# Retiling the expert stage of an mLSTM and hash-routing kernel: 416 rows for each expert, row tiles and a shared column-tiled tile

## The chip, the cores and the metric

The kernel runs on one core of a Trainium2 chip. The metric is device time in microseconds (us) of one execution. All arithmetic that matters here is f32.

## The reference

Two blocks follow each other. The first is an mLSTM cell over 4 batches, 8 heads, 768 steps and a head size of 40; its output is bridged to 3072 tokens of 320 numbers. The second sends every token to one of 8 experts, a two-layer network of 320 to 1024 to 320:

```python
def _moe_ref(x, token_ids, w1, w2):          # x 3072x320, w1 8x320x1024, w2 8x1024x320
    expert_idx = token_ids * np.int64(2654435761) % np.int64(E)
    out = np.zeros((N, D), dtype=np.float32)
    for e in range(E):
        mask = expert_idx == e
        if not mask.any():
            continue
        xe = x[mask]
        h = np.maximum(xe @ w1[e], 0.0)
        out[mask] = h @ w2[e]
    return out.astype(np.float32)
```

The multiplier is 1 modulo 8, so a token's expert is its id modulo 8. With the ids that the reference's setup draws, the experts get 405, 404, 389, 366, 385, 370, 377 and 376 tokens.

## The kernel before

**The mLSTM stage** works by chunks of 128 steps, 24 chunks in all, and writes each chunk's 128 tokens to a buffer in HBM (`x_d`). Between the chunks, routing runs in pieces: every token gets a slot (expert, rank within the expert), and a table of slots becomes two index tiles, `g_idx` (which row of `x_d` a slot reads) and `s_idx` (which row of the output it writes). `route_slots` is the piece that turns ranks into slots on VectorE. An empty slot reads row 0 and writes beyond the output, which drops it.

**The expert stage** gives each expert NJ = 4 tiles of 128 slots, 512 rows. For each expert in turn:

- `gather`: four indirect DMAs on GpSimd's queue fetch 128 rows of 320 numbers each.
- `turn`: TensorE transposes each 128x320 tile in three pieces (128, 128 and 64 columns) into PSUM; VectorE copies the two full pieces to `xT`, ScalarE the 64-row piece.
- `layer1`: for each of FB = 8 blocks of 128 hidden units, three matmuls accumulate 512 columns in one PSUM bank: contraction rows 0 to 127, 128 to 255 and the remaining 64. VectorE (even blocks) and ScalarE (odd blocks) apply the relu into `h`.
- `layer2`: for each of the 4 tiles, eight matmuls with a 128x128 piece of `h` as weights and 320 columns of `w2t` moving; ScalarE copies the result, and an indirect DMA on GpSimd's queue scatters the rows.

TensorE's program in this stage is the plain loop: `layer1(e)`, `turn(e + 1)`, `layer2(e)`, with the gathers two experts ahead and the weights three. Each f32 matmul stands in the profile as two records, each with a weight load (engine PEld) of its own; a transpose is one record. After the eight experts a loop runs over tiles of tokens beyond an expert's capacity; with the counts above it has no iteration.

Two places of the mLSTM stage are used below because they already use part of the array: `scores` (L253) multiplies from partitions 0 to 39 for even heads, then from 64 to 103 for odd heads, and `state` (L273) writes head by head to output partitions 0 to 63 and 64 to 127 in turn.

Of the kernel before, what the change touches and what calls it, by code (L numbers as in the profile page):

```python
# [8 lines left out]
F32 = mybir.dt.float32  # L9
# [4 lines left out]
AF = mybir.ActivationFunctionType  # L14
# [8 lines left out]
def kernel(  # L23
# [41 lines left out]
    NJ = 4  # L65
    CAP = NJ * P
    NX = -(-(N - CAP) // P)
    NC = E * NJ + NX

    consts = ctx.enter_context(tc.tile_pool(name="consts", bufs=1))  # L70
    wpool = ctx.enter_context(tc.tile_pool(name="wpool", bufs=3))

# [7 lines left out]
    def weights(src1, src2):  # L80
        w1t = wpool.tile([P, DB, F], F32, name="w1t")
        w2t = wpool.tile([P, FB, Dm], F32, name="w2t")
        for db, (d0, dsz) in enumerate(dch):
            nc.sync.dma_start(w1t[:dsz, db, :], src1[d0 : d0 + dsz, :])
        nc.sync.dma_start(w2t[:], src2.rearrange("(a p) d -> p a d", p=P))
        return w1t, w2t
# [6 lines left out]
    with tc.tile_pool(name="gates", bufs=1) as gp, \  # L93
# [117 lines left out]
        def decays(s):  # L211
# [27 lines left out]
            # The sigmoid is below the least normal number where this bound on its exponent matters.  # L239
# [77 lines left out]
        # The routing depends on the token ids alone: it runs in pieces between the steps above.  # L317
        iotas = {}
        for name, shape, pattern, base, mult in (
            ("experts", [P, E], [[1, E]], 0, 0),  # L320
            ("b1off", [P, E], [[CAP, E]], -1, 0),
            ("b2off", [P, E], [[-CAP, E]], E * CAP - CAP, 0),
            ("thr", [P, NX], [[P, NX]], CAP, 0),
            ("kx", [1, NX], [[1, NX]], 0, 0),
            ("iota_f", [P, P], [[1, P]], 0, 0),
            ("tokv", [P, NT], [[1, NT]], 1, NT),
        ):
# [3 lines left out]
        experts, b1off, b2off, thr, kx, iota_f, tokv = (t[1] for t in iotas.values())  # L331
# [25 lines left out]
        def route_counts():  # L357
            # 2654435761 is 1 modulo E, so the hash is the id's low bits, of either sign and with any wrap.
# [40 lines left out]
        def route_slots():  # L399
# [3 lines left out]
            nc.vector.tensor_scalar(gx[:], slot[:], scalar1=CAP + 0.5, scalar2=None, op0=ALU.is_ge)  # L403
            nc.vector.tensor_tensor(gx[:], gx[:], b2[:].unsqueeze(2).to_broadcast([P, E, NT]), op=ALU.mult)
            nc.vector.tensor_add(slot[:], slot[:], gx[:])
# [36 lines left out]
        def route_index():  # L442
            # A slot without a token reads row 0 and writes beyond the last row, which drops it.
# [32 lines left out]
    def gather(g):  # L476
        g["xg"] = xp.tile([P, NJ, Dm], F32, name="xg", bufs=3)
        for j in range(g["n"]):
            nc.gpsimd.indirect_dma_start(  # L479
                out=g["xg"][:, j, :], out_offset=None,  # L480
                in_=x_d[:, :], in_offset=bass.IndirectOffsetOnAxis(ap=g["gi"](j), axis=0),
            )

    def turn(g):
        g["xT"] = xp.tile([P, DB, CAP], F32, name="xT")
        for j in range(g["n"]):
            tp = mps.tile([P, DB, P], F32, name="tp")
            for db, (d0, dsz) in enumerate(dch):
                nc.tensor.transpose(tp[:dsz, db, :], g["xg"][:, j, d0 : d0 + dsz], ident[:])
            full = [db for db, (_, dsz) in enumerate(dch) if dsz == P]  # L490
            nf = len(full)
            cols = slice(j * P, (j + 1) * P)
            nc.vector.tensor_copy(g["xT"][:, :nf, cols], tp[:, :nf, :])  # L493
            if nf < DB:
                dsz = dch[-1][1]
                nc.scalar.copy(g["xT"][:dsz, nf, cols], tp[:dsz, nf, :])

    def layer1(g):
        cols = g["n"] * P
        g["h"] = xp.tile([P, FB, CAP], F32, name="h")  # L500
        for fb in range(FB):
            hp = mps.tile([P, CAP], F32, name="mh", bufs=3)
            for db, (_, dsz) in enumerate(dch):
                nc.tensor.matmul(  # L504
                    hp[:, :cols], lhsT=g["w"][0][:dsz, db, fb * P : (fb + 1) * P], rhs=g["xT"][:dsz, db, :cols],
                    start=(db == 0), stop=(db == DB - 1),
                )
            if fb % 2 == 0:
                nc.vector.tensor_relu(g["h"][:, fb, :cols], hp[:, :cols])  # L509
            else:  # L510
                nc.scalar.activation(g["h"][:, fb, :cols], hp[:, :cols], AF.Relu)  # L511

    def layer2(g):
        for j in range(g["n"]):
            zp = mps.tile([P, Dm], F32, name="zp")
            for fb in range(FB):
                nc.tensor.matmul(  # L517
                    zp[:], lhsT=g["h"][:, fb, j * P : (j + 1) * P], rhs=g["w"][1][:, fb, :],
                    start=(fb == 0), stop=(fb == FB - 1),
                )  # L520
            zo = xp.tile([P, Dm], F32, name="zo", bufs=4)
            nc.scalar.copy(zo[:], zp[:])  # L522
            ins = nc.gpsimd.indirect_dma_start(  # L523
                out=out[:, :], out_offset=bass.IndirectOffsetOnAxis(ap=g["si"](j), axis=0),
                in_=zo[:], in_offset=None, bounds_check=N - 1, oob_is_err=False,
            )
            ins = getattr(ins, "ins", ins)
            if g["apart"]:
                tc.declare_no_dep(ins, group="rows_out", reason="disjoint rows")
                tc.add_to_no_dep_group("rows_out", ins)  # L530
# [4 lines left out]
    with tc.manual_schedule():  # L535
        groups = [
            dict(n=NJ, w=None, gi=cols_of(g_idx, e * NJ), si=cols_of(s_idx, e * NJ), apart=True) for e in range(E)
        ]
        gather(groups[0])
        gather(groups[1])  # L540
        turn(groups[0])
        for e, g in enumerate(groups):
            if e + 2 < E:
                gather(groups[e + 2])
            g["w"] = W[e]
            layer1(g)
            if e + 1 < E:
                turn(groups[e + 1])
            layer2(g)
            if e + 3 < E:  # L550
                load_weights(e + 3)

    nx = nc.values_load(xe[0:1, NX : NX + 1], min_val=0, max_val=NX)
    with tc.If(nx > 0):
        with tc.For_i(0, nx, 1) as i:
            ex = nc.sync.value_load(xe[0:1, bass.ds(i, 1)], min_val=0, max_val=E - 1)
            gs = xp.tile([P, 2], I32, name="gs")
            nc.vector.tensor_copy(gs[:, 0:1], g_idx[:, bass.ds(i + E * NJ, 1)])
            nc.vector.tensor_copy(gs[:, 1:2], s_idx[:, bass.ds(i + E * NJ, 1)])
            g = dict(  # L560
                n=1, gi=lambda j: gs[:, 0:1], si=lambda j: gs[:, 1:2], apart=False,
                w=weights(
                    moe_w1[bass.ds(ex, 1)].rearrange("e d f -> (e d) f"),
                    moe_w2[bass.ds(ex, 1)].rearrange("e f d -> (e f) d"),
                ),
            )
            gather(g)
            turn(g)
            layer1(g)
            layer2(g)  # L570
# [30 lines left out]
```

## Time and profile before

| | us |
|---|---|
| median of 3 runs | 704.04 |
| lowest and highest run | 700.69, 704.35 |
| profiled execution: span from first to last instruction | 699.7 |
| mLSTM stage and first gathers and transposes (0 to 346.07) | 346.1 |
| expert stage, first layer-1 matmul to the end of the last layer-2 matmul (346.07 to 690.71) | 344.6 |
| last copy, last scatter and the end of the program | 9.0 |

The profile gives no other time for its execution than the span. The lowest of the runs is 1.0 us above that span and the median 4.3 us. TensorE is busy for 618.8 us of the span (88%), VectorE 255.2 (36%), GpSimd 137.5 (20%) and ScalarE 105.9 (15%). A busy TensorE counts pipelined records, so the busy share alone doesn't tell how many columns went through; for that, the starts of records are compared. The granted clock of TensorE has two levels, 0.50 (1.2 GHz) and 1.00 (2.4 GHz); its mean over the span is 0.804.

### The profile page before, as it was taken

What the parts mean: (1) busy time and instruction counts of PE and PEld (TensorE: products, weight loads), DVE (VectorE), ACT (ScalarE), POOL (GpSimd) and SP (SyncE); (2) the same over time, 40 slices, a digit from 0 to 9 for tenths busy, and PEclk for the clock granted to TensorE, in tenths of its full rate; (3) what the DMA queues carried; (4) which work ended last, traced back from release to release, by engine and by line L of the source; (5) the groups of instructions that cost most, each with busy time, mean ns of one, the idle gap of its engine ahead of it and who ended that gap; (6) DMA issues with size and microseconds to landing.
All of it is one profiled execution on the core that took longest, in us unless ns stands there. A gap on an engine that the chain in (4) does not pass through costs nothing.

```text
span 699.7 us, 7038 instructions
## 1 busy us (share of the span) xinstructions
PE 618.8 (88%) x2696; PEld 430.5 (62%) x2696; DVE 255.2 (36%) x501; ACT 105.9 (15%) x195; POOL 137.5 (20%) x190
## 2 busy tenths in 40 slices
PE   0897894568799998999499999999999999999994
PEld 0896893568799998999135446364463644536353
DVE  7477585553477877766111010110101001010000
ACT  0322120111022222221011010111101101011000
POOL 2233112221113222221511302113031130201001
PEclk9996555555555575555599999999999999999998
DMA  9235332322238888410312421223221230000000
GB/s 142 22 64 78 48 48 47 49 47 48 46 48 224 207 176 175 80 25 19 95 28 85 134 74 51 93 94 123 75 82 58 94 123 0 28 0 19 10 9 19
DMA packets 117906, 50.51 MB, mean 72 GB/s; under 512 B 102188, under 2 KB 113456, under 8 KB 117872
## 3 DMA queue, kind: packets, MB, share of 16 engines
q1 hardware_dynamic: 114560, 40.64, 27.9%
q0 software_dynamic: 3072, 9.18, 4.2%
q8 instruction: 22, 0.36, 0.2%
q10 hardware_dynamic: 240, 0.22, 0.2%
q14 instruction: 12, 0.10, 0.1%
HBM read 42.16 MB, written 9.18 MB: 73 GB/s over the span
## 4 chain that ended last, share of the span: by engine, by line
issue 44%; PE 36%; POOL 10%; DVE 7%; ACT 1%; DMA 1%; POOLq 0%; ACTq 0%; DVEq 0%
PE hp L300 11%; PE sp L253 9%; PE tr L206 6%; POOL out_dram L523 4%; POOL xg L479 4%; PE cx L266 3%; PE ab L219 2%; PE cx L273 2%; PE tk L436 2%; DVE eo L243 2%; POOL w L227 1%; ACT w L231 1%; POOL oh_c L427 1%; DVE p L255 1%; DVE w L223 1%
## 5 line engine op out<-in xcount | busy, mean ns | idle before, releaser
L504 PE MATMUL mh<-xT,w1t 128*128 128x512 f32 (+1 forms) x384 | 191.8, 630 | 0.5 <-DVE xT L493 0.5
L504 PEld LDWEIGHTS mh<-xT,w1t 128*128 128x128 f32 (+1 forms) x384 | 63.5, 189 | 125.1 <-issue 123.0
L517 PE MATMUL zp<-w2t,h 128*128 128x320 f32 x512 | 139.2, 433 | 0.0
L517 PEld LDWEIGHTS zp<-w2t,h 128*128 128x128 f32 x512 | 96.7, 190 | 40.0 <-issue 0.8
L509 DVE TENSOR_SCALAR h<-mh 128x512 f32<-128x512 f32 x32 | 22.1, 691 | 268.1 <-PE mh L504 268.1
L523 POOL DMA_INDIRECT out_dram<-zo,s_idx x32 | 31.6, 988 | 283.2 <-ACT zo L522 283.2
L300 PE MATMUL hp<-v,p 128*128 128x41 f32 x384 | 78.5, 386 | 2.0 <-DVE p L255 2.0
L300 PEld LDWEIGHTS hp<-v,p 128*128 128x128 f32 x384 | 75.6, 300 | 3.5 <-DVE p L255 2.4
L227 POOL TENSOR_SCALAR_AFFINE_SELECT w<-w 128x512 f32<-128x512 f32 x48 | 31.4, 678 | 229.1 <-DVE w L223 229.1
L253 PE MATMUL sp<-kqT 40*128 40x128 f32 x384 | 70.3, 420 | 0.0
L253 PEld LDWEIGHTS sp<-kqT 40*128 40x128 f32 x384 | 63.4, 308 | 1.9 <-ACT kqT L209 0.2
L209 ACT COPY kqT<-tr 128x512 f32<-128x512 f32 x48 | 28.0, 586 | 175.4 <-PE tr L206 175.4
L243 DVE RECIPROCAL eo<-eo 128x320 f32<-128x320 f32 x24 | 51.7, 2152 | 0.8
L206 PE MATMUL tr<-ident,kq 128*128 128x128 f32 x192 | 46.3, 418 | 0.0
L511 ACT ACTIVATE h<-mh 128x512 f32<-128x512 f32 x32 | 19.1, 597 | 172.9 <-PE mh L504 172.9
L206 PEld LDWEIGHTS tr<-ident,kq 128*128 128x128 f32 x192 | 36.9, 218 | 5.2 <-issue 5.1
L436 PE MATMUL tk<-oh_c,oh_r 128*128 128x52 f32 x48 | 11.2, 420 | 29.2 <-POOL oh_c L427 29.2
L223 DVE TENSOR_TENSOR w<-ab,e_T 128x512 f32<-128x512 f32 x48 | 30.8, 682 | 15.4 <-PE ab L219 15.4
L479 POOL DMA_INDIRECT xg<-x_rows,g_idx x32 | 31.1, 971 | 25.5 <-issue 24.6
L266 PE MATMUL cx<-C,kqT 128*128 128x82 f32 x160 | 35.6, 397 | 0.1
L231 ACT ACTIVATE w<-w 128x1024 f32<-128x1024 f32 x24 | 25.4, 1057 | 65.4 <-POOL w L227 65.4
L266 PEld LDWEIGHTS cx<-C,kqT 128*128 128x128 f32 x160 | 33.6, 309 | 0.5 <-issue 0.5
(134 smaller groups left out, 369.0 us busy)
## 6 DMA issues: line engine op xcount, KB each, us to landing
w2t<-in_moe_w_dram SPq DMA_DIRECT2D x8, 1280.0 KB, 6.6
w1t<-in_moe_w_dram SPq DMA_DIRECT2D x16, 512.0 KB, 4.6
kq<-in_k_dram SPq DMA_DIRECT2D x24, 160.0 KB, 3.3
kq<-in_q_dram SPq DMA_DIRECT2D x24, 160.0 KB, 4.2
v<-in_v_dram SPq DMA_DIRECT2D x24, 160.0 KB, 4.4
o_sb<-in_o_gate_dram SPq DMA_DIRECT2D x24, 160.0 KB, 4.1
x_rows<-x SPq DMA_DIRECT2D x24, 160.0 KB, 1.9
w1t<-in_moe_w_dram SPq DMA_DIRECT2D x8, 256.0 KB, 5.6
```

Of the source, the lines that this page charges most:

```text
L206: nc.tensor.transpose(tp[:, j, :], d["kq"][:, i, 2 * j : 2 * j + 2, :].rearrange("p h d -> p (h d)"), ident[:],)
L223: nc.vector.tensor_tensor(w[:, hf], ab[:], e_T[:, c, b * H + hf : (b + 1) * H : 2].unsqueeze(2).to_broadcast([P, PR, P]), op=ALU.add,)
L227: nc.gpsimd.affine_select(w[:, hf], w[:, hf], compare_op=ALU.is_ge, fill=NEG, base=0, pattern=[[0, PR], [1, P]], channel_multiplier=-1,)
L231: nc.scalar.activation(w[:], w[:], AF.Exp)
L243: nc.vector.reciprocal(d["eo"][:], d["eo"][:])
L253: nc.tensor.matmul(sp[:, j, :], lhsT=kqT[r, 0, j, :], rhs=kqT[r, 1, j, :], start=True, stop=True)
L266: nc.tensor.matmul(cx[:, 2 * j * D1 : (2 * j + 2) * D1], lhsT=d["kqT"][:, 1, j, :], rhs=st["C"][:, j].rearrange("p h d -> p (h d)"), start ...
L300: nc.tensor.matmul(hp[:, h, :], lhsT=d["p"][h % 2][:, h // 2, :], rhs=d["v"][:, h, :], start=True, stop=True)
L479: nc.gpsimd.indirect_dma_start(out=g["xg"][:, j, :], out_offset=None, in_=x_d[:, :], in_offset=bass.IndirectOffsetOnAxis(ap=g["gi"](j), ax ...
L504: nc.tensor.matmul(hp[:, :cols], lhsT=g["w"][0][:dsz, db, fb * P : (fb + 1) * P], rhs=g["xT"][:dsz, db, :cols], start=(db == 0), stop=(db ...
L517: nc.tensor.matmul(zp[:], lhsT=g["h"][:, fb, j * P : (j + 1) * P], rhs=g["w"][1][:, fb, :], start=(fb == 0), stop=(fb == FB - 1),)
L523: ins = nc.gpsimd.indirect_dma_start(out=out[:, :], out_offset=bass.IndirectOffsetOnAxis(ap=g["si"](j), axis=0), in_=zo[:], in_offset=None ...
```

## The change

Capacity and tiles. An expert has NJ = 3 tiles of 128 slots and 32 more (RM). Four experts (EG) share one tile of 128 slots for their 32-slot remainders. The overflow loop begins beyond 416 tokens. `route_slots` has two limits in place of one, so four more VectorE instructions.

Transposes. The last 64 columns of a gathered tile are duplicated by a VectorE copy, so that the third transpose is 128 wide and puts the 64 remainder rows on partitions 0 to 63 and again on 64 to 127. One copy, in turn by VectorE and ScalarE, takes all three pieces out of PSUM. The shared remainder tile is turned once for each four experts, and GpSimd copies an expert's 32 columns of it into `xT`.

Layer 1. Hidden blocks go in pairs. The 64-row remainder of the contraction comes first, for the even block from partitions 0 to 63 and for the odd one from 64 to 127 (`w1c` holds the weights in that layout); then four full matmuls of 416 columns.

Layer 2. Three tiles for each expert. GpSimd copies the last 32 columns of `h` to `hrem`. After the fourth and the eighth expert, `rest` multiplies: for each hidden block, four matmuls with 32 columns of weights each, one for each expert, which write 32 output partitions each of one PSUM tile.

Weights. `w1t` and `w1c` have three buffers, `w2t` six.

```diff
-    NJ = 4
-    CAP = NJ * P
+    NJ = 3
+    RM = 32
+    EG = P // RM
+    NM = NJ * P
+    CAP = NM + RM
...
+        w1t = wpool.tile([P, 2, F], F32, name="w1t")
+        w1c = wpool.tile([P, FB // 2, P], F32, name="w1c")
+        w2t = w2pool.tile([P, FB, Dm], F32, name="w2t")
...
+            rank = gp.tile([P, E, NT], F32, name="rank")
+            nc.vector.tensor_copy(rank[:], slot[:])
+            for cap, off in ((NM, rmoff), (CAP, b2)):
+                nc.vector.tensor_scalar(gx[:], rank[:], scalar1=cap + 0.5, scalar2=None, op0=ALU.is_ge)
...
+    def turn(xg, dst, on_act):
+        tp = mps.tile([P, DB, P], F32, name="tp")
+        for db in range(2):
+            nc.tensor.transpose(tp[:, db, :], xg[:, db * P : (db + 1) * P], ident[:])
+        nc.vector.tensor_copy(xg[:, Dm:], xg[:, 2 * P : Dm])
+        nc.tensor.transpose(tp[:, 2, :], xg[:, 2 * P :], ident[:])
+        if on_act:
+            nc.scalar.copy(dst, tp[:])
+        else:
+            nc.vector.tensor_copy(dst, tp[:])
+
+    def layer1(w, xT, h, cols):
+        w1t, w1c, _ = w
+        for fp in range(FB // 2):
+            hp = [mps.tile([P, CAP], F32, name="mh", bufs=4) for _ in range(2)]
+            for i in range(2):
+                r = slice(i * P // 2, (i + 1) * P // 2)
+                nc.tensor.matmul(hp[i][:, :cols], lhsT=w1c[r, fp, :], rhs=xT[r, 2, :cols], start=True, stop=False)
+            for i in range(2):
+                fb = 2 * fp + i
+                for db in range(2):
+                    nc.tensor.matmul(
+                        hp[i][:, :cols], lhsT=w1t[:, db, fb * P : (fb + 1) * P], rhs=xT[:, db, :cols],
+                        start=False, stop=(db == 1),
+                    )
...
+        def turns(e):
+            xT = xTs[e] = xp.tile([P, DB, CAP], F32, name="xT")
+            for j in range(NJ):
+                turn(xgs[e][:, j, :], xT[:, :, j * P : (j + 1) * P], j % 2 == 1)
+            if e % EG == 0:
+                remT[e // EG] = xp.tile([P, DB, P], F32, name="remT")
+                turn(xgs[-1 - e // EG], remT[e // EG][:], True)
+            i = e % EG
+            nc.gpsimd.tensor_copy(xT[:, :, NM:], remT[e // EG][:, :, i * RM : (i + 1) * RM])
+
+        def rest(g):
+            zp = mps.tile([P, Dm], F32, name="zp")
+            for fb in range(FB):
+                for i in range(EG):
+                    nc.tensor.matmul(
+                        zp[i * RM : (i + 1) * RM, :], lhsT=hrem[g][:, i, fb, :], rhs=W[g * EG + i][2][:, fb, :],
+                        start=(fb == 0), stop=(fb == FB - 1),
+                    )
+            scatter(zp, cols_of(s_idx, NR + g)(0), True)
...
+            layer1(W[e], xTs[e], h, CAP)
+            nc.gpsimd.tensor_copy(hrem[g][:, i], h[:, :, NM:])
+            if e + 1 < E:
+                turns(e + 1)
+            layer2(W[e], h, NJ, cols_of(s_idx, e * NJ), True)
+            if i == EG - 1:
+                rest(g)
```

How the instructions stand on the engines follows from this. Line numbers in the rows of after are those of the changed file; a multiplier counts equal instructions in a row.

TensorE, before, from the last transposes of a turn to the next expert's first ones (L489 transposes, L517 layer 2, L504 layer 1):

```order
L489 MATMUL tp<-ident,xg 128x128 x2
L489 MATMUL tp<-ident,xg 64x128
L517 MATMUL zp<-w2t,h 128x320 x32
L504 MATMUL mh<-xT,w1t 128x512 x24
L489 MATMUL tp<-ident,xg 128x128 x2
```

All 32 matmuls of layer 2 use the whole array; the eight of layer 1 that multiply the 64-row remainder stand alone between full ones.

TensorE, now, from the turn of the shared remainder tile behind the fourth expert's layer 1 to the fifth expert's layer 1 (L512 and L514 transposes, L543 layer 2, L578 the shared tile, L526 the row-tiled remainder, L530 full matmuls):

```order
L512 MATMUL tp<-ident,xr 128x128 x2
L514 MATMUL tp<-ident,xr 128x128
L543 MATMUL zp<-w2t,h 128x320 x24
L578 MATMUL zp<-w2t,hrem 32x320 x32
L526 MATMUL mh<-xT,w1c 128x416 x2
L530 MATMUL mh<-xT,w1t 128x416 x4
```

Layer 2 has 24 matmuls for 32, and 32 narrow ones follow after the fourth and the eighth expert. Two remainders stand side by side, once for two hidden blocks.

VectorE, before, at the end of the mLSTM stage and in the first turn (L314 the last chunk's output, L493 transposed tile to `xT`, L509 relu):

```order
L310 RECIPROCAL den<-den 128x8
L311 TENSOR_TENSOR x<-hx,den 128x320
L314 TENSOR_TENSOR x<-x,eo 128x320
L493 COPY xT<-tp 128x2x128 x4
L509 TENSOR_SCALAR h<-mh 128x512 x4
```

Nothing on VectorE stands between a gather and a transpose there.

VectorE, now, at the same place (L325 the last chunk's output, L513 the 64-column copy, L518 transposed tile to `xT`, L535 relu):

```order
L325 TENSOR_TENSOR x<-x,eo 128x320
L513 COPY xg<-xg 128x64
L518 COPY xT<-tp 128x3x128
L513 COPY xg<-xg 128x64 x2
L518 COPY xT<-tp 128x3x128
L513 COPY xr<-xr 128x64
L535 TENSOR_SCALAR h<-mh 128x416 x4
```

The second tile's 64-column copy, for which TensorE's third transpose of that tile waits, stands behind the first tile's copy out of PSUM. In later turns the order is the same, without the shared tile's row except in the turn for the fifth expert. On GpSimd the copy of the remainder columns into the first expert's `xT` stands behind seven gathers (four of the first expert, three of the second) and ahead of the third expert's; before, twelve gathers stood there in a row.

## Rows read from the trace of the kernel before

**Rows 1.** Busy time by stretch: us, engines' busy (count), granted clock, DMA share, GB/s

```profile
346.07:350.45 4.38, 4.37 (x5) 1.67 (x6) 0.00 (x0) 0.25 (x1) 3.42 (x4) 0.50 0.51 128
350.60:690.71 340.11, 335.97 (x976) 166.63 (x974) 32.69 (x60) 39.58 (x91) 51.28 (x53) 1.00 0.19 61
180.00:240.00 60.00, 59.83 (x376) 56.71 (x376) 40.93 (x82) 12.94 (x20) 12.65 (x17) 0.56 0.60 128
```

**Rows 2.** TensorE's timeline over one expert: start, us, work [idle before]

```profile
391.23 23.70 PE L504 MATMUL mh<-xT,w1t 128*128 128x512 f32 x48
414.86 0.88 PE L489 MATMUL tp<-ident,xg 128*128 128x128 f32 x6
416.29 0.88 PE L489 MATMUL tp<-ident,xg 128*128 128x128 f32 x6 [0.55 <-ACT xT L496]
417.00 17.39 PE L517 MATMUL zp<-w2t,h 128*128 128x320 f32 x64
434.23 23.70 PE L504 MATMUL mh<-xT,w1t 128*128 128x512 f32 x48
```

**Rows 3.** Timeline of weight loads in layer 1, a little over one hidden block

```profile
440.60 0.19 PEld L504 LDWEIGHTS mh<-xT,w1t 128*128 128x128 f32 x1 [0.24 <-issue]
441.02 0.19 PEld L504 LDWEIGHTS mh<-xT,w1t 128*128 128x128 f32 x1 [0.24 <-issue]
441.97 0.29 PEld L504 LDWEIGHTS mh<-xT,w1t 64*128 64x128 f32 x2 [0.76 <-issue]
443.02 0.30 PEld L504 LDWEIGHTS mh<-xT,w1t 128*128 128x128 f32 x2 [0.76 <-issue]
443.56 0.19 PEld L504 LDWEIGHTS mh<-xT,w1t 128*128 128x128 f32 x1 [0.24 <-issue]
```

**Rows 4.** TensorE's timeline in an mLSTM chunk at the full clock

```profile
255.72 0.67 PE L273 MATMUL cx<-v,kw 128*64 128x41 f32 x16
256.31 1.98 PE L300 MATMUL hp<-v,p 128*128 128x41 f32 x16
258.22 1.71 PE L253 MATMUL sp<-kqT 40*128 40x128 f32 x16
```

**Rows 5.** The same, window from 255.700 to 255.724

```profile
255.51 0.28 PE L266 MATMUL cx<-C,kqT 128*128 128x82 f32 x1
255.72 0.26 PE L273 MATMUL cx<-v,kw 128*64 128x41 f32 x2
```

**Rows 6.** Timeline of all engines where the expert stage begins

```profile
344.86 0.95 POOL L479 DMA_INDIRECT xg<-x_rows,g_idx  x1 [0.30 <-issue]
345.60 0.42 DVE L493 COPY xT<-tp 128x256 f32<-128x256 f32 x1 [1.43 <-PE tp L489]
346.08 2.08 PE L504 MATMUL mh<-xT,w1t 128*128 128x512 f32 x2 [0.52 <-DVE xT L493]
```

**Rows 7.** Groups by line: operation, shapes, count | busy us, mean ns | idle before

```profile
L209 ACT COPY kqT<-tr 128x512 f32<-128x512 f32 x48 | 28.0, 586 | 175.4 <-PE tr L206 175.4
L522 ACT COPY zo<-zp 128x320 f32<-128x320 f32 x32 | 13.6, 426 | 122.5 <-PE zp L517 122.5
L509 DVE TENSOR_SCALAR h<-mh 128x512 f32<-128x512 f32 x32 | 22.1, 691 | 268.1 <-PE mh L504 268.1
L438 DVE COPY tv<-tk 128x52 f32<-128x52 f32 x1 | 0.2, 213 | 3.5 <-PE tk L436 3.5
L346 POOL CAST iota_f<-iota_f_i 128x128 f32<-128x128 int32 x1 | 0.3, 289 | 0.1
L427 POOL TENSOR_TENSOR oh_c<-oh_c,tokv 128x312 f32<-128x312 f32 x4 | 5.1, 1286 | 15.9 <-DVE oh_c L423 15.9
```

**Rows 8.** VectorE's timeline in the routing piece that numbers the slots

```profile
101.44 0.26 DVE L403 TENSOR_SCALAR gx<-slot 128x192 f32<-128x192 f32 x1
101.73 0.36 DVE L404 TENSOR_TENSOR gx<-gx,b 128x192 f32<-128x192 f32 x1
102.13 0.36 DVE L405 TENSOR_TENSOR slot<-slot,gx 128x192 f32<-128x192 f32 x1
```

More of the change, by code (lines that the diff above doesn't have):

```diff
@@ L63 @@
     DB = len(dch)
-    NJ = 4
-    CAP = NJ * P
+    NJ = 3
[3 more added lines that the diff above has]
+    CAP = NM + RM
+    NR = E * NJ
     NX = -(-(N - CAP) // P)
-    NC = E * NJ + NX
+    NC = NR + E // EG + NX
+    assert DB == 3 and dch[-1][1] == P // 2 and FB % 2 == 0 and E % EG == 0
     consts = ctx.enter_context(tc.tile_pool(name="consts", bufs=1))
     wpool = ctx.enter_context(tc.tile_pool(name="wpool", bufs=3))
+    w2pool = ctx.enter_context(tc.tile_pool(name="w2pool", bufs=EG + 2))
     x_d = nc.dram_tensor("x_rows", (N, Dm), F32, kind="Internal").ap()
@@ L80, in weights @@
     def weights(src1, src2):
[L81 to L84, printed above, removed]
+        w1t = wpool.tile([P, 2, F], F32, name="w1t")
+        w1c = wpool.tile([P, FB // 2, P], F32, name="w1c")
+        w2t = w2pool.tile([P, FB, Dm], F32, name="w2t")
+        nc.sync.dma_start(w1t[:], src1[: 2 * P, :].rearrange("(a p) f -> p a f", p=P))
+        last = src1[2 * P :, :].rearrange("d (a two f) -> two d a f", two=2, f=P)
+        for i in range(2):
+            nc.sync.dma_start(w1c[i * P // 2 : (i + 1) * P // 2], last[i])
         nc.sync.dma_start(w2t[:], src2.rearrange("(a p) d -> p a d", p=P))
-        return w1t, w2t
+        return w1t, w1c, w2t
     W = {}
@@ L320 @@
             ("experts", [P, E], [[1, E]], 0, 0),
[L321 to L322 removed]
+            ("b1off", [P, E], [[NM, E]], -1, 0),
+            ("rmoff", [P, E], [[RM - NM, E]], NR * P - NM, 0),
+            ("b2off", [P, E], [[-RM, E]], E * RM - RM, 0),
             ("thr", [P, NX], [[P, NX]], CAP, 0),
@@ L330 @@
             )
-        experts, b1off, b2off, thr, kx, iota_f, tokv = (t[1] for t in iotas.values())
+        experts, b1off, rmoff, b2off, thr, kx, iota_f, tokv = (t[1] for t in iotas.values())
         lt_strict = gp.tile([P, P], F32, name="lt_strict")
@@ L474 @@
     mps = ctx.enter_context(tc.tile_pool(name="mps", bufs=2, space=PSUM))
[L476 to L511, printed above, removed]
@@ L513, in layer2, with gather, scatter @@
-    def layer2(g):
-        for j in range(g["n"]):
+    def gather(xg, idx):
+        nc.gpsimd.indirect_dma_start(
+            out=xg, out_offset=None, in_=x_d[:, :], in_offset=bass.IndirectOffsetOnAxis(ap=idx, axis=0),
+        )
+    def scatter(zp, idx, apart):
+        zo = xp.tile([P, Dm], F32, name="zo", bufs=4)
+        nc.scalar.copy(zo[:], zp[:])
+        ins = nc.gpsimd.indirect_dma_start(
+            out=out[:, :], out_offset=bass.IndirectOffsetOnAxis(ap=idx, axis=0),
+            in_=zo[:], in_offset=None, bounds_check=N - 1, oob_is_err=False,
+        )
+        ins = getattr(ins, "ins", ins)
+        if apart:
+            tc.declare_no_dep(ins, group="rows_out", reason="disjoint rows")
+            tc.add_to_no_dep_group("rows_out", ins)
@@ new lines, in turn @@
+    def turn(xg, dst, on_act):
[15 more added lines that the diff above has]
+                nc.tensor.matmul(hp[i][:, :cols], lhsT=w1c[r, fp, :], rhs=xT[r, 2, :cols], start=True, stop=False)
+            for i in range(2):
+                fb = 2 * fp + i
[3 more added lines that the diff above has]
+                        start=False, stop=(db == 1),
+                    )
+                if i == 0:
+                    nc.vector.tensor_relu(h[:, fb, :cols], hp[i][:, :cols])
+                else:
+                    nc.scalar.activation(h[:, fb, :cols], hp[i][:, :cols], AF.Relu)
@@ L515, in layer2 @@
+    def layer2(w, h, n, idx, apart):
+        for j in range(n):
             zp = mps.tile([P, Dm], F32, name="zp")
@@ L517, in layer2 @@
                 nc.tensor.matmul(
-                    zp[:], lhsT=g["h"][:, fb, j * P : (j + 1) * P], rhs=g["w"][1][:, fb, :],
+                    zp[:], lhsT=h[:, fb, j * P : (j + 1) * P], rhs=w[2][:, fb, :],
                     start=(fb == 0), stop=(fb == FB - 1),
                 )
[L521 to L530, printed above, removed]
+            scatter(zp, idx(j), apart)
     def cols_of(t, c0):
@@ L535, with fetch @@
     with tc.manual_schedule():
[L536 to L542, printed above, removed]
-            if e + 2 < E:
-                gather(groups[e + 2])
-            g["w"] = W[e]
-            layer1(g)
+        xgs, xTs, remT, hrem = {}, {}, {}, {}
+        def fetch(e):
+            if e % EG == 0:
+                xgs[-1 - e // EG] = xp.tile([P, DB * P], F32, name="xr")
+            xgs[e] = xp.tile([P, NJ, DB * P], F32, name="xg", bufs=3)
+            for j in range(NJ):
+                gather(xgs[e][:, j, :Dm], cols_of(g_idx, e * NJ)(j))
+            if e % EG == 0:
+                gather(xgs[-1 - e // EG][:, :Dm], cols_of(g_idx, NR + e // EG)(0))
@@ new lines, in turns @@
+        def turns(e):
+            xT = xTs[e] = xp.tile([P, DB, CAP], F32, name="xT")
+            for j in range(NJ):
+                turn(xgs[e][:, j, :], xT[:, :, j * P : (j + 1) * P], j % 2 == 1)
+            if e % EG == 0:
+                remT[e // EG] = xp.tile([P, DB, P], F32, name="remT")
[9 more added lines that the diff above has]
+                        start=(fb == 0), stop=(fb == FB - 1),
+                    )
+            scatter(zp, cols_of(s_idx, NR + g)(0), True)
@@ L547 @@
+        fetch(0)
+        fetch(1)
+        turns(0)
+        for e in range(E):
+            g, i = e // EG, e % EG
+            if e + 2 < E:
+                fetch(e + 2)
+            h = xp.tile([P, FB, CAP], F32, name="h")
+            if i == 0:
+                hrem[g] = xp.tile([P, EG, FB, RM], F32, name="hrem")
+            layer1(W[e], xTs[e], h, CAP)
+            nc.gpsimd.tensor_copy(hrem[g][:, i], h[:, :, NM:])
             if e + 1 < E:
-                turn(groups[e + 1])
-            layer2(g)
+                turns(e + 1)
+            layer2(W[e], h, NJ, cols_of(s_idx, e * NJ), True)
+            if i == EG - 1:
+                rest(g)
@@ L554 @@
     with tc.If(nx > 0):
-        with tc.For_i(0, nx, 1) as i:
-            ex = nc.sync.value_load(xe[0:1, bass.ds(i, 1)], min_val=0, max_val=E - 1)
+        with tc.For_i(0, nx, 1) as k:
+            ex = nc.sync.value_load(xe[0:1, bass.ds(k, 1)], min_val=0, max_val=E - 1)
             gs = xp.tile([P, 2], I32, name="gs")
[L558 to L565, printed above, removed]
-            )
[L567 to L570, printed above, removed]
+            nc.vector.tensor_copy(gs[:, 0:1], g_idx[:, bass.ds(k + (NC - NX), 1)])
+            nc.vector.tensor_copy(gs[:, 1:2], s_idx[:, bass.ds(k + (NC - NX), 1)])
+            w = weights(
+                moe_w1[bass.ds(ex, 1)].rearrange("e d f -> (e d) f"),
+                moe_w2[bass.ds(ex, 1)].rearrange("e f d -> (e f) d"),
+            )
+            xr = xp.tile([P, DB * P], F32, name="xr")
+            xT = xp.tile([P, DB, CAP], F32, name="xT")
+            h = xp.tile([P, FB, CAP], F32, name="h")
+            gather(xr[:, :Dm], gs[:, 0:1])
+            turn(xr, xT[:, :, :P], False)
+            layer1(w, xT, h, P)
+            layer2(w, h, 1, lambda j: gs[:, 1:2], False)
 _INS = ['q', 'k', 'v', 'i_gate', 'f_gate', 'o_gate', 'moe_token_ids', 'moe_w1', 'moe_w2']
```

5 lines of the change are left out of this document (2 added, 3 removed).

## The prediction

> **What bounds the kernel now.** I read the busy table by stretch first. From the first layer-1 matmul to the last layer-2 matmul TensorE is busy nearly without a gap and has the full 2.4 GHz from 350.5 us on [rows 1]; GpSimd, VectorE and ScalarE are busy for a sixth of that time or less, and the relu's engine waits 268.1 us for TensorE [rows 7]. So the expert stage, 344.6 us of the 699.7 us span, lasts as long as TensorE's records take. Next the timeline of one expert: layer 1 takes 414.86 - 391.23 = 23.63 us, the turn 2.14, layer 2 434.23 - 417.00 = 17.23 [rows 2]. Then the cost of one record. Layer 2 has 64 records in 17.23 us, 0.269 us each: 320 columns at 0.833 ns (two passes of 2.4 GHz) are 0.267, so records follow each other without loss. In layer 1 two plain records start 441.02 - 440.60 = 0.42 us apart, which is 512 columns at the same rate plus 2 ns; but a whole hidden block, 23.63/8, takes 2.954, and six records only 6 x 0.429 (512 x 0.833 + 2 ns) = 2.574. The other 0.38 us lie at the two changes between the full and the 64-row array: there the weight load is no longer ahead of the matmul, and the step from 441.02 to 441.97 holds two records in 0.95, the one from 443.02 to 443.56 one in 0.54 [rows 3].
>
> **Layer 1.** A record of 416 columns takes 416 x 0.833 + 2 = 0.349 us. A pair of hidden blocks now has four full matmuls, eight records, and two remainder matmuls, four records, on different halves of the partitions. The question is whether these two run at once. The trace has the case: the scores multiply from partitions 0 to 39 in eight records, then from 64 to 103 in eight. Sixteen records of 128 columns one after the other would need 15 x 0.107 + 0.28 for the last one to come through (as the whole-array record of [rows 5]), and two slow starts of 0.1 us (a quarter of the 0.38 above), together 2.1; the group takes 1.71 [rows 4], so the second half began before the first was through. I take full overlap: 2 x 0.349 for the pair. With the two array changes once for two blocks, 10 x 0.349 + 0.38 = 3.87 us, four times 15.48. That is 8.15 us less for each expert, 65.2 for eight.
>
> **Layer 2.** 48 records of 0.269 are 12.92, which is 4.31 less, 34.5 for eight experts.
>
> **The shared tile.** 64 records of 320 columns for each four experts, on four strips of 32 output columns. The state matmuls show two strips of 64: in a window of 24 ns two of their records begin [rows 5]; sixteen end after 0.67 us where the next line's whole-array records of the same 41 columns need 1.98 [rows 4]. One record lasts 0.26 [rows 5], so the sixteen starts lie within 0.67 - 0.26 = 0.41, 27 ns apart, while the streaming of one takes 41 x 0.833 = 34. So two strips do stream at once. Four are not in the trace. Bounds: all four at once, 16 x 0.269 = 4.3 us; none, 64 x 0.269 = 17.2. I take the first, by the nearest row, and 0.3 for the array changes: 4.6 twice, 9.2.
>
> The Trainium skill (TensorE: Matmul & The Clock Gate, Part 3, table of measured speedups) gives 3.07 and not 4 for four row tiles and 2.38 for three column tiles. No run here shows four. By 3.07 of 4, the shared tiles would cost 2.6 us more in all and the remainder pairs, if they lost as much, 6.8 us; an estimate from that page, and inside my range.
>
> **The turns.** The 64-column copy costs about as much as a 52-column VectorE copy, 0.21 [rows 7]. The PSUM copy of 384 numbers is on VectorE 0.69 x 384/512 and a little, 0.55, and on ScalarE between 0.43 for 320 and 0.59 for 512, 0.48 [rows 7]. TensorE does five transposes of 0.11, then the second tile's third one waits for the first tile's copy and the 64-column copy behind it: about 1.4 us after the start; the third tile follows, and layer 2 starts after 1.9, against 2.14, which had a stall of 0.55 of its own [rows 2]. The turn before the fifth expert has the shared tile too and waits twice more: 3.0. Six times -0.25 and once +0.9 is -0.6. If the copies ran in half the time or twice, the stage would move by 3 us at most.
>
> **Where the stage begins.** The first layer-1 matmul waited for VectorE's copy, which ended at 346.02 [rows 6]. Now it waits for ScalarE's copy of the shared tile and then for GpSimd's copy, which stands behind the seventh gather: that began at 344.86 and took 0.95 [rows 6]. The copy of 96 numbers costs between 0.29 (the cast of 128) and 1.29 (a product of 312) [rows 7]; I take 0.35, since it is the smaller piece. So +0.6. The first 4.4 us of layer 1 ran at half clock [rows 1]; if the clock rises at the same moment, a later start loses less there, and +0.3 is left. GpSimd's other copies and the DMAs lie beside 28 us of TensorE for each expert. Weights are asked for three experts ahead as before.
>
> **Routing.** Four more VectorE instructions over 192 numbers: two like the 0.26 row, two like the 0.36 rows, with gaps 1.35 us [rows 8]. VectorE is in the chain there, so I count them in full. The table shrinks from 52 to 47 columns: GpSimd's product of 1.29 us becomes 0.12 shorter, four times, and VectorE's a little: -0.65. Net +0.7. A shift there can also move the windows in which the mLSTM stage had the full clock; that may be 3 us either way.
>
> **Sum.** -65.2 - 34.5 + 9.2 - 0.6 + 0.3 + 0.7 = -90.1: a span of 699.7 - 90.1 = 609.6. The median of the runs is 4.3 above the profiled span, so 614. Clock windows, turns and the spread of the runs give this case 607 to 621.
>
> **Rivals.** First, *records overlap only with their neighbours*. Each f32 matmul is two records, and in strict order the second of one tile stands ahead of the first of the next. A pair then takes three records' time and not two: 0.349 x 4 x 8 = 11.2 more; four strips take 4 x 2 records less the overlapping half: 32 x 0.269 = 8.6 for each shared tile in place of 4.3, 8.6 more in all. 634. For it speaks that the second half of the scores began only near the end of the first; against it the two records within 24 ns, since one record streams for 34 ns and its twin on the same strip can't begin sooner. The Trainium skill (the same page, Part 3, What overlaps and what doesn't) states this order, matmuls starting and ending strictly in sequence; this trace disagrees, as far as rows 5 reach.
>
> Second, *no overlap*: +22.3 in layer 1 (64 records of 0.349) and +25.8 in the shared tiles (96 of 0.269): 662. The scores speak against it, and it is still faster than before, because 512 rows became 416.
>
> Third, the other side: *the clock falls*. From 180 to 240 us TensorE is busy for 59.83 of 60 us, and the granted clock is 0.56 [rows 1]: being busy isn't enough. If the tiled pairs, the waits in the turns and the narrow matmuls made the expert stage run at 1.2 GHz, its 254 us would double, to 866. It decides from 90 us on that run at half clock. Against it: the mLSTM's records are short ones, 41 columns (34 ns of streaming) in 1.98/16 = 0.12 us [rows 4], while the new layer 1 streams columns for 3.49 of 3.87 us, a greater share than the old 2.57 of 2.95, and layer 2 is unchanged in kind.
>
> That the capacity of 416 is exceeded, and the overflow loop runs, is excluded by the token counts, 405 at most.
>
> **Chances.** The forecast 0.78, neighbours only 0.12, no overlap 0.05, the clock 0.04, and 0.01 for a time like before's. The first two together reach from 607 to 634; with what four strips may lose and the spread, 606 to 637 holds eight in ten. What differs by under 0.5%, 3.5 us, counts as no change, about what runs of this kernel can tell: faster 0.95, same 0.01, slower 0.04.
>
> **What would show it.** In the new profile, layer 1 should take 15.5 us for each expert, layer 2 12.9, the 64 records of a shared tile 4.3, and two remainder records should begin within 10 ns of each other. Layer 1 of 16.9 says neighbours only, of 18.3 no overlap; a shared tile of 8.6 means two strips at once. The turns should show VectorE's 64-column copy as what ended TensorE's waits. A granted clock under 0.95 after the stage's first 5 us would make the prediction wrong from the other side, and so would a TensorE wait for GpSimd or a weight DMA of more than 1 us for each expert.

## The result and the profile after

The changed kernel takes 610.36 us (median of 6 runs, 606.01 to 610.94), the kernel before 701.57 (6 runs, 700.69 to 704.35): a ratio of 0.868, with a 95% interval from 0.864 to 0.871. The forecast of 614 lies 3.6 us above it. The profiled execution took 606.11 us, with a span of 604.4, against 699.7 before; it is one of the two short runs of the six, the other four took 610.29 to 610.94.

The busy table by stretch answers to [rows 1]. The first two rows are the expert stage, divided where the clock rises; the third is what comes after the last matmul. Columns as there.

```profile
342.80:349.20 6.40, 6.40 (x11) 3.02 (x12) 0.59 (x1) 0.00 (x0) 2.90 (x3) 0.50 0.36 105
349.40:596.57 247.17, 242.55 (x952) 137.54 (x950) 28.89 (x67) 31.00 (x65) 44.91 (x56) 1.00 0.25 80
596.57:604.40 7.83, 0.00 (x1) 0.00 (x0) 0.00 (x0) 0.42 (x1) 0.97 (x1) 0.84 0.00 0
```

TensorE is nearly as full as before, 242.55 of 247.17 us, and its clock stays at 2.4 GHz until the last matmul has ended: the third rival did not come. The stage is shorter because fewer columns go through one after the other. TensorE's timeline over a layer 1, a turn and a layer 2 answers to [rows 2] (start, us, work, idle before and its releaser):

```profile
376.22 0.97 PE L526 MATMUL mh<-xT,w1c 64*128 64x416 f32 x4
377.12 3.06 PE L530 MATMUL mh<-xT,w1t 128*128 128x416 f32 x8
380.11 0.97 PE L526 MATMUL mh<-xT,w1c 64*128 64x416 f32 x4
...
391.68 0.38 PE L512 MATMUL tp<-ident,xg 128*128 128x128 f32 x2
391.90 0.27 PE L514 MATMUL tp<-ident,xg 128*128 128x128 f32 x1
392.01 0.38 PE L512 MATMUL tp<-ident,xg 128*128 128x128 f32 x2
393.00 0.33 PE L514 MATMUL tp<-ident,xg 128*128 128x128 f32 x1 [0.60 <-DVE xg L513]
393.16 0.38 PE L512 MATMUL tp<-ident,xg 128*128 128x128 f32 x2
393.38 0.27 PE L514 MATMUL tp<-ident,xg 128*128 128x128 f32 x1
393.49 13.09 PE L543 MATMUL zp<-w2t,h 128*128 128x320 f32 x48
406.50 0.97 PE L526 MATMUL mh<-xT,w1c 64*128 64x416 f32 x4
```

Starts are compared: layer 1 takes 391.68 - 376.22 = 15.46 us for 23.63, the turn 1.81 for 2.14, layer 2 406.50 - 393.49 = 13.01 for 17.23. The four remainder records of a pair take 0.90 us from their first to the next matmul (376.22 to 377.12), where four one after the other would need 1.40. The turn's one wait is the one foreseen: the second tile's third transpose stands for 0.60 us until VectorE's 64-column copy is done, which comes behind the copy out of PSUM (VectorE's timeline in that turn):

```profile
392.28 0.56 DVE L518 COPY xT<-tp 128x384 f32<-128x384 f32 x1 [1.10 <-PE tp L514]
392.75 0.36 DVE L513 COPY xg<-xg 128x64 f32<-128x64 f32 x2
```

The shared tile, on the same timeline, and two short windows that answer to [rows 5], one of 20 ns where a remainder pair begins, one of 30 ns where the shared tile begins:

```profile
455.20 13.09 PE L543 MATMUL zp<-w2t,h 128*128 128x320 f32 x48
468.22 4.51 PE L578 MATMUL zp<-w2t,hrem 128*32 128x320 f32 x64
472.66 0.62 PE L526 MATMUL mh<-xT,w1c 64*128 64x416 f32 x2
```

```profile
376.22 0.62 PE L526 MATMUL mh<-xT,w1c 64*128 64x416 f32 x2
```

```profile
468.22 0.48 PE L578 MATMUL zp<-w2t,hrem 128*32 128x320 f32 x4
```

Two records begin together, one on each half, and four, one on each strip (the rows don't name the half or the strip; records of one half start 0.35 us or more apart, as the run with one half shows below); 64 records need 472.66 - 468.22 = 4.44 us, which is 16 x 0.269 and 0.13 that I put down to the change of array shape.

Where the stage begins, from the last write of the mLSTM stage on (all engines, then TensorE alone up to the first turn):

```profile
330.93 0.32 SPq L326 DMA_DIRECT2D x_rows<-x  x1
341.94 0.48 ACT L516 COPY remT<-tp 128x384 f32<-128x384 f32 x1 [2.11 <-PE tp L514]
342.48 0.26 POOL L572 COPY xT<-remT 128x96 f32<-128x96 f32 x1
```

```profile
342.80 1.76 PE L526 MATMUL mh<-xT,w1c 64*128 64x416 f32 x4 [0.90 <-POOL xT L572]
361.43 0.38 PE L512 MATMUL tp<-ident,xg 128*128 128x128 f32 x2
```

Term by term, in us of the two profiled spans (stages by the starts of their first records):

| term | predicted | measured |
|---|---|---|
| layer 1, seven warm experts | -57.1 (seven times -8.15) | -57.1 (15.47 for 23.63) |
| layer 1, first expert | -8.15, and about -0.3 for less time at half clock | -7.2 (18.63 for 25.86) |
| layer 2 | -34.5 | -34.0 |
| shared tiles | +9.2 | +9.0 (4.44 and 4.51) |
| seven turns | -0.6 | -1.5 (15.3 to 13.8) |
| last write of the mLSTM stage to first layer-1 matmul | +0.6 | +0.1 (11.74 to 11.87) |
| mLSTM stage, routing included | +0.7 | -3.4 (334.3 to 330.9, start of its last write) |
| after the last matmul | 0 | -1.2 (9.0 to 7.8) |
| sum | -90.1 | -95.3 |

### The profile page after: what moved, and what is told of

It reads as the page before. It is cut to its first block, busy times and chain, and to the rows that moved or that the text cites. A ratio compares the mean times of both kernels' runs of the same rounds, so it can differ in the third digit from the quotient of the medians.

```text
span 604.4 us, 6995 instructions
## 1 busy us (share of the span) xinstructions
PE 518.1 (86%) x2678; PEld 393.3 (65%) x2678; DVE 253.5 (42%) x515; ACT 97.0 (16%) x167; POOL 130.7 (22%) x196
## 5 line engine op out<-in xcount | busy, mean ns | idle before, releaser
L543 PE MATMUL zp<-w2t,h 128*128 128x320 f32 x384 | 104.7, 432 | 0.0
L535 DVE TENSOR_SCALAR h<-mh 128x416 f32<-128x416 f32 x32 | 18.9, 592 | 196.0 <-PE mh L530 196.0
L530 PE MATMUL mh<-xT,w1t 128*128 128x416 f32 x256 | 100.3, 536 | 0.0
L543 PEld LDWEIGHTS zp<-w2t,h 128*128 128x128 f32 x384 | 72.5, 190 | 29.4 <-issue 0.3
L530 PEld LDWEIGHTS mh<-xT,w1t 128*128 128x128 f32 x256 | 47.1, 194 | 51.5 <-issue 51.5
L311 PEld LDWEIGHTS hp<-v,p 128*128 128x128 f32 x384 | 72.2, 288 | 7.6 <-DVE p L266 6.6
L499 POOL DMA_INDIRECT out_dram<-zo,s_idx x26 | 25.6, 985 | 102.3 <-ACT zo L498 102.3
L451 PE MATMUL tk<-oh_c,oh_r 128*128 128x47 f32 x48 | 11.2, 429 | 32.2 <-POOL oh_c L442 32.2
L234 DVE TENSOR_TENSOR w<-ab,e_T 128x512 f32<-128x512 f32 x48 | 30.8, 682 | 12.0 <-PE ab L230 11.9
L537 ACT ACTIVATE h<-mh 128x416 f32<-128x416 f32 x32 | 16.5, 517 | 112.4 <-PE mh L530 112.4
L526 PE MATMUL mh<-xT,w1c 64*128 64x416 f32 x128 | 31.8, 574 | 0.9 <-POOL xT L572 0.9
```

What stands on the lines that cost most here:

```text
L234: nc.vector.tensor_tensor(w[:, hf], ab[:], e_T[:, c, b * H + hf : (b + 1) * H : 2].unsqueeze(2).to_broadcast([P, PR, P]), op=ALU.add,)
L311: nc.tensor.matmul(hp[:, h, :], lhsT=d["p"][h % 2][:, h // 2, :], rhs=d["v"][:, h, :], start=True, stop=True)
L499: ins = nc.gpsimd.indirect_dma_start(out=out[:, :], out_offset=bass.IndirectOffsetOnAxis(ap=idx, axis=0), in_=zo[:], in_offset=None, bound ...
L526: nc.tensor.matmul(hp[i][:, :cols], lhsT=w1c[r, fp, :], rhs=xT[r, 2, :cols], start=True, stop=False)
L530: nc.tensor.matmul(hp[i][:, :cols], lhsT=w1t[:, db, fb * P : (fb + 1) * P], rhs=xT[:, db, :cols], start=False, stop=(db == 1),)
L543: nc.tensor.matmul(zp[:], lhsT=h[:, fb, j * P : (j + 1) * P], rhs=w[2][:, fb, :], start=(fb == 0), stop=(fb == FB - 1),)
```

## The experiments

All of them change the kernel after, but for the last of the first four, which changes the kernel before. All ran on one chip; the kernel before took 699.1 us there beside the first four (one run) and 701.32 (median of 9) beside the others. Each variant but the last is a single run. The stages are read from the traces, because whole runs also differ by the mLSTM stage, of which more below.

**One half only.** Both remainder matmuls of a pair multiply from partitions 0 to 63.

```diff
...
-                r = slice(i * P // 2, (i + 1) * P // 2)
-                nc.tensor.matmul(hp[i][:, :cols], lhsT=w1c[r, fp, :], rhs=xT[r, 2, :cols], start=True, stop=False)
+                r = slice(0, P // 2)
+                nc.tensor.matmul(hp[i][:, :cols], lhsT=w1c[r, 2 * fp + i, :], rhs=xT[r, 2, :cols], start=True, stop=False)
```

> Both remainder matmuls of a pair of hidden blocks multiply from partitions 0 to 63; the rest is the changed kernel. Theory 1 (two halves of the array run at once): their four records now follow each other, two more of 0.349 us for each pair, so layer 1 takes 15.47 + 4 x 0.70 = 18.26 us for each expert and the span grows by 22.3 us. Theory 2 (records overlap only with their neighbours): one record more for each pair, 16.86 us and 11.2 us. Theory 3 (the halves did not overlap and the gain came from 416 rows alone): no change.

630.79 us. TensorE's timeline from one layer 1 to the turn behind it:

```profile
381.53 1.66 PE L524 MATMUL mh<-xT,w1c 64*128 64x416 f32 x4
383.12 3.06 PE L528 MATMUL mh<-xT,w1t 128*128 128x416 f32 x8
386.11 1.66 PE L524 MATMUL mh<-xT,w1c 64*128 64x416 f32 x4
...
399.76 0.27 PE L510 MATMUL tp<-ident,xg 128*128 128x128 f32 x1
```

The four remainder records now take 1.59 us (381.53 to 383.12) for 0.90, and layer 1 takes 18.23: theory 1 said 18.26, theory 2 16.86. The overlap of the halves is complete, and worth 8 x 2.77 = 22.1 us of the gain.

**Strip by strip.** In the shared tile the two loops are exchanged.

```diff
-            for fb in range(FB):
-                for i in range(EG):
+            for i in range(EG):
+                for fb in range(FB):
```

> In the shared tile the loops are exchanged: all eight hidden blocks of one expert's strip of 32 output columns, then the next expert's. Theory 1 (TensorE issues in order and looks only a few records ahead, as the scores of the first stage suggested, where the second half began three records before the end of the first): strips overlap only where one follows the other, so 64 records take 64 x 0.269 less three boundaries of about three records, 14.8 us for each shared tile in place of 4.4 to 4.5, and the span grows by about 20.7 us. Theory 2 (each strip runs by itself, however far ahead): no change, 4.4. Theory 3 (no look ahead at all): 17.2 us and 25.5.

627.59 us. TensorE's timeline:

```profile
470.21 14.27 PE L578 MATMUL zp<-w2t,hrem 128*32 128x320 f32 x64
484.41 0.97 PE L526 MATMUL mh<-xT,w1c 64*128 64x416 f32 x4
```

A shared tile takes 14.20 us, close to the 14.8 of theory 1. In the single records of the trace the second strip's first one starts 6 ns after the thirteenth of the first strip's sixteen. A window of 30 ns there shows the twelfth, the thirteenth and that one:

```profile
473.19 0.73 PE L578 MATMUL zp<-w2t,hrem 128*32 128x320 f32 x3
```

Three more of the first strip have still to start at that moment, as in the scores of the mLSTM stage. So a strip's records can start ahead of another strip's that stand before them in the program, but only a few records ahead. The order in `rest`, in which the strip changes with every matmul, is what makes the strips run together throughout; by this run it is worth 9.8 us for each tile, 19.5 in all.

**Remainders side by side.** The first pair of blocks has its full matmuls first, the second its remainders first, and so on.

```diff
-        for fp in range(FB // 2):
...
+        for f0 in range(0, FB // 2, 2):
...
+            full(f0)
+            part(f0)
+            part(f0 + 1)
...
+            full(f0 + 1)
```

> In layer 1 the first pair of hidden blocks has its full matmuls first and its 64-row remainders last, the second pair its remainders first, and so on, so two pairs' remainders stand together and the array changes shape four times for each expert and not eight times. Theory 1 (each change there and back costs 0.38 us, whatever stands between): layer 1 falls from 15.47 to 14.71 us and the span by 6.1 us. Theory 2 (the cost belongs to each remainder matmul and not to the change of shape): no change.

602.45 us. TensorE's timeline over one layer 1 and the layer 2 behind it:

```profile
377.83 2.96 PE L535 MATMUL mh<-xT,w1t 128*128 128x416 f32 x8
380.72 1.67 PE L527 MATMUL mh<-xT,w1c 64*128 64x416 f32 x8
382.32 5.85 PE L535 MATMUL mh<-xT,w1t 128*128 128x416 f32 x16
388.10 1.67 PE L527 MATMUL mh<-xT,w1c 64*128 64x416 f32 x8
389.70 3.06 PE L535 MATMUL mh<-xT,w1t 128*128 128x416 f32 x8
392.60 0.38 PE L512 MATMUL tp<-ident,xg 128*128 128x128 f32 x2
...
394.40 13.09 PE L563 MATMUL zp<-w2t,h 128*128 128x320 f32 x48
407.32 0.51 PE L535 MATMUL mh<-xT,w1t 128*128 128x416 f32 x1
```

Eight remainder records take 1.60 us, and four took 0.90: the 0.70 between are two times 0.349 for the second pair, and the 0.20 left of the 0.90 belong to the change of shape. Layer 1 takes 14.77 and layer 2 12.92, together 0.80 less for each expert (0.7 for the fourth, fifth and eighth, next to the shared tiles), as theory 1 has it: the price is on the change of shape and not on the matmul.

**Row tiles alone.** The kernel before, with its 512 rows, gets the row-tiled layer 1, the wide third transpose and the weights in two halves (`weights`, `turn` and `layer1` as in the change's diff), but no 416 rows and no shared tile.

> The kernel before, with 512 rows for each expert and no shared tile, and of the change only the row tiles in layer 1 with the transposes they need. By the terms of the sum: ten records of 0.429 and 0.38 for each pair of blocks, so layer 1 takes 18.7 us in place of 23.63, 39.5 less in all, and the four-tile turns 2.3 to 3.5 in place of 2.14, up to 9 us more: a span of 660 to 670 us. If the row tiles were worth as little as 3.07 of 4, layer 1 would be at 19.7.

668.41 us, of which 666.6 are span. TensorE's timeline over one expert:

```profile
388.29 1.13 PE L511 MATMUL mh<-xT,w1c 64*128 64x512 f32 x4
389.35 3.70 PE L515 MATMUL mh<-xT,w1t 128*128 128x512 f32 x8
392.98 1.13 PE L511 MATMUL mh<-xT,w1c 64*128 64x512 f32 x4
...
406.96 0.38 PE L494 MATMUL tp<-ident,xg 128*128 128x128 f32 x2
...
409.22 0.44 PE L494 MATMUL tp<-ident,xg 128*128 128x128 f32 x2 [0.30 <-ACT xT L498]
409.68 0.33 PE L496 MATMUL tp<-ident,xg 128*128 128x128 f32 x1
409.84 2.59 PE L528 MATMUL zp<-w2t,h 128*128 128x320 f32 x9
```

Layer 1 takes 406.96 - 388.29 = 18.67 us, the expected 18.7; the four-tile turn 2.88. Row tiles are worth 5.0 us for each expert here, less 0.75 for a longer turn. So the larger part of the change's 91 us, about 60, comes with the smaller number of rows, 416 for 512, which pays in layer 2 (34.0 us) because the shared tiles are cheap (9.0). An estimate for a layer 1 of 416 rows, from the experiments' own prices: of the 8.16 us that it became shorter, 2.77 are the overlap (one half only), 4 x 0.38 = 1.5 the halved number of shape changes, and the other 3.9 the rows.

**The 64-column copies first.** In a turn they stand ahead of the copies out of PSUM (`widen` is the copy), and the third tile, and the shared one, goes to a bank of layer 1.

```diff
...
+    def turn(xg, dst, on_act, own):
+        if own:
+            tp = mps.tile([P, DB, P], F32, name="tp")[:]
+        else:
+            tp = mps.tile([P, CAP], F32, name="mh", bufs=4)[:, : DB * P].rearrange("p (a b) -> p a b", b=P)
...
             for j in range(NJ):
-                turn(xgs[e][:, j, :], xT[:, :, j * P : (j + 1) * P], j % 2 == 1)
+                widen(xgs[e][:, j, :])
...
```

> In a turn all 64-column copies stand ahead of the copies out of PSUM on VectorE, and the third tile (and the shared one) is transposed into a bank of layer 1. Theory 1 (the turn's stall is the second tile's third transpose waiting for the 64-column copy behind the first PSUM copy): a turn falls from 1.80 to 1.84 us to about 1.05, the one with the shared tile from 2.91 to about 1.36, and the span by 6.2 us. Theory 2 (TensorE would then wait for a free PSUM tile or for the relu's engines in place of it): turns of 1.6 us or more, under 2 us in all.

603.62 us. TensorE's timeline of a turn, six transposes into the tiles of before and three into the bank of layer 1:

```profile
394.87 0.82 PE L517 MATMUL tp<-ident,xg 128*128 128x128 f32 x6
395.53 0.49 PE L517 MATMUL mh<-ident,xg 128*128 128x128 f32 x3
395.85 1.51 PE L546 MATMUL zp<-w2t,h 128*128 128x320 f32 x5
```

The turn takes 0.98 us for 1.81, the one with the shared tile 1.31 for 2.91, 6.6 less in all seven. With both edits no wait is left in the turn. The wait that the trace of after names, 4.3 us in all, was the queue order on VectorE; how much of the rest is the extra bank was not tried apart.

**A warm start.** Eleven matmuls whose result nobody reads stand ahead of, between and behind the first expert's transposes (`WARM` is 7).

```diff
+        def warm(n):
+            for _ in range(n):
+                wp = mps.tile([P, CAP], F32, name="mh", bufs=4)
+                nc.tensor.matmul(wp[:], lhsT=ident[:], rhs=W[0][0][:, 0, :CAP], start=True, stop=True)
...
+                if e == 0:
+                    warm(1)
...
+        warm(WARM)
         turns(0)
+        warm(1)
```

> Eleven matmuls of 416 columns whose result nobody reads stand between the mLSTM stage and the first expert: seven ahead of the first transposes, one behind each tile's. Theory 1 (the first expert's layer 1 lost 1.7 to 3.7 us in four profiles because it began at 1.2 GHz after TensorE had waited for the first rows): the clock rises ahead of layer 1, which then takes 15.5 us for the first expert too, and the time from the last write of the mLSTM stage to the first layer-1 matmul stays at 11.9 us or a little less. Theory 2 (these matmuls delay the transposes as much as they give): layer 1 at 15.5, but a start that is 2 us or more later.

605.02 us. The clock rose 3 us after the first of them. The busy table from the first of them to the first layer-1 matmul and over the first layer 1:

```profile
331.38:344.87 13.49, 11.57 (x34) 5.54 (x35) 3.44 (x11) 0.96 (x2) 7.17 (x8) 0.89 0.31 86
344.90:360.30 15.40, 15.40 (x48) 7.06 (x49) 2.47 (x5) 1.55 (x3) 2.90 (x3) 1.00 0.15 43
```

The first expert's layer 1 now takes 15.47 us too, at a granted clock of 1.00; in the five other profiles without these matmuls (after, one half, strip by strip, side by side, the copies first) it took 1.7 to 3.6 us more than the later ones of the same kernel. The time from the last write of the mLSTM stage to the first layer-1 matmul was 11.8 us, against 11.9 in after.

**All three together.** One kernel with three of the edits above: remainders side by side, copies first, warm start.

> The adjacent remainders, the early 64-column copies and the eleven matmuls together. If the three terms are independent, 0.80 for each expert, 6.2 in the turns and about 3 at the first expert: 15.6 us below the changed kernel's median of 610.4, 595 us. If the turns' gain is lost to the other order of relus (the last pair of blocks still ends with its full matmuls, so I expect no such loss), 601.

593.33 us, median of 5 runs (592.71 to 595.33), against 701.32 for the kernel before on the same chip: a ratio of 0.846, from 0.845 to 0.848, clear of the change's own 0.868. The three terms add up: in the traces the stage from the first layer-1 matmul to the end of the last matmul falls from 253.77 to 238.04 us, 15.7 less where 15.6 were expected; the medians differ by 17.0. This version beats both kernels.

**What whole runs can't tell.** The first layer-1 matmul, behind an mLSTM stage whose code is the same, started at 342.80 (after), 344.86 (one half), 346.29 (strip by strip), 346.68 (side by side), 347.92 (copies first), 344.87 (warm start) and 347.75 (all three), a spread of 5.1 us, and at 346.08 in the kernel before. As far as the profiles show, it goes with when and how long the clock was at 2.4 GHz in the stage: in the profile of after for 44 us, from 42 us on, in that of before for 27, from 53 on, in copies first for 20. The length alone doesn't order them: strip by strip has 44 us too, but none before 107 us, and its fourth chunk was written at 79.97 us against 77.20 in after. What sets those windows I did not try to find, and no run tests the link. The profiles' mean clocks don't help here: the stretch ahead of the first clock record counts as full speed, but in the kernel before the sixteen records of L300 took 3.64 us at 43.5 us, ahead of its first clock record, against 1.98 at 2.4 GHz [rows 4]. The routing term can still be read, from the writes at both ends of the piece in which the slots are numbered (SyncE's queue, after):

```profile
91.99 0.35 SPq L326 DMA_DIRECT2D x_rows<-x  x1
106.57 0.34 SPq L326 DMA_DIRECT2D x_rows<-x  x1
```

14.58 us, against 13.19 in the kernel before; 14.57 and 14.56 in the first two experiments, and 13.2 again in the one with the routing of before.

## Why the prediction was right

**What bounds the stage** was read rightly: TensorE's records, at a rate that the trace of before showed, and nothing else came to bind. The relu's engine still waits for TensorE (196.0 us in the stage), as do the scatters through ScalarE's copies.

**Layer 1** was foreseen to 0.02 us (15.48 and 15.47). The doubtful step was that both halves run at once. The run with one half confirms it by its cost, and the two records within the 20 ns window show it directly. *Neighbours only* needed 16.9 and is out; *no overlap* 18.3 is what the run with one half gives.

**The shared tile** was 4.6 each and is 4.44 and 4.51. Here the prediction went from two strips [rows 5] to four without a row for four, and that held. The Trainium skill's measured speedup of 3.07 for four row tiles (TensorE: Matmul & The Clock Gate, Part 3, Measured speedup vs the span model) would make about 5.6, an estimate from that figure; by this trace four column strips give 64 x 0.269/4.44 = 3.9. The Trainium skill's rule that matmuls start and end strictly in program order (the same page, Part 3, What overlaps and what doesn't) is also not what the traces show: four matmuls of two records each stand in a row, and the first record of each starts within the 30 ns window; in the run strip by strip the second strip's first record starts ahead of the first strip's last three. The rival that followed from it had its grain of truth in the queue: with all of one strip's matmuls first, the overlap is lost but for a few records.

**Layer 2** was 0.1 us too low for each expert, since part of a change of shape falls into its stretch, which the prediction had counted in layer 1 alone; side by side, where layer 1 begins with full matmuls, layer 2 takes the predicted 12.92.

**The turns**: the wait, its place and its releaser were right; a turn is 0.05 to 0.1 shorter than worked out, since VectorE's copies overlap: the 64-column copy starts at 392.75, 0.09 us ahead of the end of the copy before it. That makes 0.6 of the 0.9 us by which the sum missed; the other 0.3 is that the seven turns of before took 15.3 us and not seven times 2.14 (one took 2.51).

**The begin of the stage**: the GpSimd copy took 0.26 us and not 0.35, and ScalarE's copy ended in the same moment as the seventh gather (342.42), so neither added to the other. The prediction's own rows give less than its +0.6: the seventh gather's end at 345.81 and 0.35 make 346.16, 0.14 after the 346.02 of before, and 0.1 was measured. But the clock rose 6.5 us after the first layer-1 matmul and not 4.4, which cost 0.9 more than before in place of 0.3 less. The warm start shows that this is all that slowed the first expert.

**Routing**: the four VectorE instructions cost the 1.35 us that they were given (14.58 - 13.19 = 1.39), and this was the chain. The smaller table gave back 0.3 (79.9 us for four chunks against 80.2), not 0.65.

**What was not in the sum**: the unchanged rest of the mLSTM stage was 4.5 us shorter, more than the 3 us that the prediction allowed its clock windows and less than their spread of 5.1 above, and the end of the program 1.2 us shorter.

**What put the forecast 3.6 us too high** is for 2.5 us none of these but the way from the span to the run: the prediction added 4.3 us, the distance of the first three runs' median to the profiled span. A run is 1.7 to 2.0 us longer than its own span in every run of both kernels for which both are known (606.11 and 604.4, 699.1 and 697.2); the profiled execution of before was then a run of some 701.5, an estimate. By 609.6 + 1.8 the forecast would have been 611.4. The other 1 us or so is the span: the predicted 609.6 stands against 608.6 to 609.2 in the four longer runs and 604.4 in the profiled one. That the forecast came so close to the median is in part luck, since the six runs of this one kernel lie up to 4.9 us apart.

## What to carry to other kernels

Before a change to a TensorE-bound stage, look in the trace for a place where the array is already used in parts, and read from starts and ends of its records whether the parts run together; that settles whether the overlap can be had before anything is built. When matmuls on parts of the array are to overlap, alternate the part from one matmul to the next, and put matmuls of one shape side by side, since each change of shape there and back cost 0.38 us here, part of it a weight load that no longer stands ahead of its matmul [rows 3]. And look in the queue of an engine with time to spare for the one short copy that the bound engine waits for: moved ahead of the longer ones, with one more bank for the results, it gave 6.6 us.

## What the runs showed of the hardware that had not been expected

Four strips of 32 output columns stream at once with almost no loss: 64 f32 records of 320 columns in 4.44 us, where 16 at the whole-array rate need 4.31. In the trace's single records the four strips' first ones start 6 to 7 ns apart.

How far ahead TensorE starts records of another part of the array is little, and the same in both places where I looked: the next strip's first record starts with the thirteenth of sixteen, and in the scores the second half's with the fifth of eight, each time 6 ns after it and with three of the earlier part still to start.

The same mLSTM code took between 342.8 and 347.9 us to the first layer-1 matmul in profiles of one kernel and of its variants; differences under 1% between two kernels with such a stage are better read from the stage that was changed.
